# A depthwise convolution whose middle tap is added by a transfer, in an FFT mixing and gated convolution kernel

## The chip, the cores and the metric

The kernel runs on one core of a Trainium2 chip. The metric is the time of one execution on the device in microseconds, as the median of several runs. One further execution was taken with the hardware profiler; its trace is what the profile views below show.

## The reference

For each of 8 batches, the input of 3136 positions by 256 features is transformed by a two-dimensional Fourier transform, of which the real part is kept. A feed-forward block with a gate follows, all in float32:

```python
X = np.fft.fft(np.fft.fft(x, axis=1), axis=2).real      # (8, 3136, 256)
h = np.maximum(X @ w_in, 0.0)                            # (8, 3136, 1024)
conv = sum(conv_w[k] * shifted(h, k) for k in range(3))  # per feature, along the positions, zeros outside
out = (h / (1.0 + np.exp(-conv))) @ w_out                # (8, 3136, 256)
```

## The kernel before, in words

The kernel folds the sequence by the symmetries of the transform (VectorE adds and subtracts halves of the input tile `xh` into `w`), multiplies the folded input with cosine and sine tables (TensorE, PSUM tile `pd`), and gets for each batch two tables `pt` and `qt` (`PQ[b]`) of 128 rows. The transform along the features and `w_in` are multiplied into one matrix `G` at the start.

The main loop has 256 steps: 8 batches, 4 chunks of positions in a batch, 8 blocks of 128 hidden features in a chunk. A step `t` works on one block of one chunk, with positions along the free axis: 770 columns of `h` to convolve, 832 in the last chunk. A chunk holds a stretch of positions and its mirror image, since the two share products.

What one step does, in the order of the data:

- `seed` (ACT, line 748) writes a rank-one term into the PSUM tile `pa`; there are two of these tiles.
- `products` (TensorE, lines 768 to 771) multiplies `G` with `qt` into `pb` (one tile) and with `pt` onto `pa`.
- `copies` (ACT, line 784) takes `pb` with both signs into `nb`.
- `row_of` (line 762) gets a tile for `h`; in chunk 0 GpSimd sets its two edge columns to zero with a memset.
- `combine` (VectorE, line 795) adds `pa` and `nb` and cuts at zero, in two halves: that is `h`.
- `first_tap` (ACT, line 801) writes `g`, the first of the three products of the convolution.
- `tap` (VectorE, line 806) adds the second and the third product, one instruction each.
- `sigmoid` (ACT, line 821) takes `g` in two pieces.
- `gate` (lines 829 and 830) multiplies `g` by `h`: GpSimd one half of the columns, VectorE the other.
- `keep` (ACT, line 837) stores the last 64 columns of a batch in `left`, so that two batches share one matmul for them.
- `mm2` (TensorE, line 849) multiplies `g` with `w_out` and sums over the 8 blocks in the PSUM tiles `po`; after the eighth, ACT copies them to `os` and SP's queue stores them.

A step `third` (lines 754 to 756), in which VectorE has side work at the start, spares VectorE one half of `combine`: TensorE adds the sum in PSUM with one more product, ACT takes the half out (line 781), and in those steps the gate is cut 3 to 1 in place of 1 to 1 two steps ahead.

The order of work on each engine is written out by hand, in the loop at the end (lines 1016 to 1047). In cycle `t` the engines get: the sigmoid of step t-2, products and copies of t+1, the products with `w_out` of t-3, combine and first tap of t, the seed of t+2, the second and third tap of t-1 and the gate of t-2. Every engine takes its instructions in this order and waits in place for what it needs.

Side work is put into the cycles by name (`side`): the folds of the next batch on VectorE, the products with the tables on TensorE (`pd`), small edge copies on GpSimd (line 178), loads of the next batch's input. Of a batch's input, SP's queue loads two halves of 784 KB and GpSimd issues eight gathers of mirrored rows (line 131). In the first cycles the weights are turned from 64-bit to 32-bit floats on VectorE and ACT.

Of the kernel before, what the change touches and what calls it, by code (L numbers as in the profile page):

```python
# [9 lines left out]
F32 = mybir.dt.float32  # L10
I32 = mybir.dt.int32
U32 = mybir.dt.uint32
AF = mybir.ActivationFunctionType
ALU = mybir.AluOpType
# [16 lines left out]
NQ = 8  # L31
CUTS = (0, 384, 768, 1152)
BIG = 3.4028234663852886e38


@with_exitstack
def kernel(
# [10 lines left out]
    nc = tc.nc  # L48
    B, S, D = x.shape
    F = moe_w_in.shape[1]  # L50
    P = 128
# [9 lines left out]
    NF = F // P  # L61
# [6 lines left out]
    const = ctx.enter_context(tc.tile_pool(name="const", bufs=1))  # L68
# [4 lines left out]
    ebp = ctx.enter_context(tc.tile_pool(name="ebp", bufs=4))  # L73
    asp = ctx.enter_context(tc.tile_pool(name="asp", bufs=4))
    pqp = ctx.enter_context(tc.tile_pool(name="pqp", bufs=2))
    hp = ctx.enter_context(tc.tile_pool(name="hp", bufs=4))
    gp = ctx.enter_context(tc.tile_pool(name="gp", bufs=5))
    nbp = ctx.enter_context(tc.tile_pool(name="nbp", bufs=2))
    osp = ctx.enter_context(tc.tile_pool(name="osp", bufs=3))
    edp = ctx.enter_context(tc.tile_pool(name="edp", bufs=1, space=DRAM))  # L80
# [5 lines left out]
    vt = nc.vector.tensor_tensor  # L86
    gt = nc.gpsimd.tensor_tensor
    stt = nc.vector.scalar_tensor_tensor
    act = nc.scalar.activation

    def mm(o, l, r, start, stop):
        nc.tensor.matmul(o, l, r, start=start, stop=stop, skip_group_check=True)  # L92

    def spare():

        return pso.tile([P, 2, D], F32, name="po", tag="po").rearrange("p a d -> p (a d)")
# [611 lines left out]
    cw = const.tile([P, 3, NF], F32, name="cw")  # L708
# [12 lines left out]
    def column(i):  # L721

        w, p = w4[i], spare()
        for m in range(NF // 4):
            for t in range(2):
                mm(p[:, m:m + 1], w[:, t, m * P:(m + 1) * P], dm[:, t, 1, P - 1:P], t == 0, t == 1)
        nc.scalar.copy(out=ge[:, i * NF // 4:(i + 1) * NF // 4], in_=p[:, 0:NF // 4])

    def taps():
        p = spare()  # L730
        mm(p[:, 0:3 * NF], cw24[:, 0], ident, True, True)
        nc.scalar.copy(out=cw.rearrange("p k m -> p (k m)"), in_=p[:, 0:3 * NF])


    rows = out.rearrange("b s d -> (b s) d")
    hs, gs, pa, pb, po, nb = {}, {}, {}, {}, {}, {}
# [6 lines left out]
    def seed(s):  # L743

        b, c, f = s
        ch, n, fs = cut(s)
        pa[s] = psa.tile([P, 512], F32, name="pa", tag="pa")
        act(pa[s][:, 0:n], eb[b, c], AF.Copy, scale=ge[:, f:f + 1])  # L748

    def triple(s):  # L750

        return third(steps.index(s))

    def third(i):

        return 3 <= i < 12 and (i, "dve") in side

    def row_of(s):
        hs[s] = hp.tile([P, HW], F32, name="h", tag="h")
# [4 lines left out]
    def products(s):  # L764
        b, c, f = s
        ch, n, fs = cut(s)
        pb[s] = psb.tile([P, 512], F32, name="pb", tag="pb")
        mm(pb[s][:, 0:n], G[0:P - 1, 1, fs], PQ[b][1][0:P - 1, ch.k0:ch.k1], True, True)
        mm(pa[s][:, 0:n], G[:, 0, fs], PQ[b][0][:, ch.k0:ch.k1], False, not triple(s))
        if triple(s):  # L770
            mm(pa[s][:, 0:n], G[0:P - 1, 1, fs], PQ[b][1][0:P - 1, ch.k0:ch.k1], False, True)

    def copies(s):

        ch, n, fs = cut(s)
        p = pb.pop(s)
        nb[s] = nbp.tile([P, 2, HN], F32, name="nb", tag="nb")
        if triple(s):
            act(nb[s][:, 1, ch.cols], p[:, ch.cols], AF.Copy, scale=-2.0)
            row_of(s)  # L780
            act(hs[s][:, ch.front], pa[s][:, ch.fcols], AF.Relu)
        else:
            for i, cols in enumerate((ch.fcols, ch.cols)):
                act(nb[s][:, i, cols], p[:, cols], AF.Copy, scale=-1.0 if i else 1.0)  # L784

    def combine(s):

        ch, n, fs = cut(s)
        a, c = pa.pop(s), nb.pop(s)
        if not triple(s):  # L790
            row_of(s)
        h = hs[s]
        for i, (to, cols) in enumerate(((h[:, ch.front], ch.fcols), (h[:, ch.back][:, ::-1], ch.cols))):
            if i or not triple(s):
                nc.vector._custom_dve(TENSOR_ADD_SAT, out=to, in0=a[:, cols], in1=c[:, i, cols],  # L795
                                      s0=BIG, s1=0.0)

    def first_tap(s):
        n = chunks[s[1]].w - 2
        gs[s] = gp.tile([P, HW - 2], F32, name="g", tag="g")[:, 0:n]  # L800
        act(gs[s], hs[s][:, 0:n], AF.Copy, scale=cw[:, 0, s[2]:s[2] + 1])  # L801

    def tap(s, k):
        g, h, f = gs[s], hs[s], s[2]
        n = g.shape[1]
        stt(out=g, in0=h[:, k:k + n], scalar=cw[:, k, f:f + 1], in1=g, op0=ALU.mult, op1=ALU.add)  # L806

    def shares(s):


        ch = chunks[s[1]]
        w = ch.w - 2
        n = ch.rest[0] if ch.last else w
        m = n - n // (4 if third(steps.index(s) + 2) else 2)
        return slice(0, m), slice(m, n), slice(n, w)

    def sigmoid(s):

        v, p, r = shares(s)
        for c in (slice(p.start, r.stop), v):  # L820
            act(gs[s][:, c], gs[s][:, c], AF.Sigmoid)  # L821

    def gate(s):

        b, c, f = s
        g, h = gs[s], hs.pop(s)[:, 1:]
        v, p, r = shares(s)
        p = slice(p.start, r.stop)
        gt(g[:, p], g[:, p], h[:, p], op=ALU.mult)  # L829
        vt(g[:, v], g[:, v], h[:, v], op=ALU.mult)  # L830

    def keep(s):

        b, c, f = s
        r = shares(s)[2]
        if r.start < r.stop:
            nc.scalar.copy(out=left[:, f, b % 2 * LEFT:(b % 2 + 1) * LEFT], in_=gs[s][:, r])

    def mm2(s):
        b, c, f = s  # L840
        ch = chunks[c]
        tiles = [(gs[s][:, o:o + m], [(0, b, r, m)]) for o, r, m in ch.tiles]
        if ch.last and b % 2:
            tiles.append((left[:, f], [(i * LEFT, b - 1 + i, ch.rest[1], LEFT) for i in range(2)]))
        for i, (w, to) in enumerate(tiles):
            if f == 0 and i % 2 == 0:
                po[b, c, i // 2] = pso.tile([P, 2, D], F32, name="po", tag="po")
            pt = po[b, c, i // 2]
            mm(pt[:, i % 2, :], w, wout[:, f, :], f == 0 and i % 2 == 0, f == NF - 1)
            if f == NF - 1 and (i % 2 or i == len(tiles) - 1):  # L850
                del po[b, c, i // 2]
                osb = osp.tile([P, 2, D], F32, name="os", tag="os")
                for j in range(i - i % 2, i + 1):
                    nc.scalar.copy(out=osb[:, j % 2], in_=pt[:, j % 2])  # L854
                    for p0, b_, r, m in tiles[j][1]:
                        nc.sync.dma_start(out=rows[b_ * S + r:b_ * S + r + m, :], in_=osb[p0:p0 + m, j % 2])
        gs.pop(s)


    w_cv.narrow(0, 1)  # L860
    taps()
    idle = psb.tile([P, 512], F32, name="pb", tag="pb")

# [48 lines left out]
    n = chunks[0].k1  # L912
# [9 lines left out]
    steps = [(b, c, f) for b in range(B) for c in range(len(chunks)) for f in range(NF)]  # L922
    per = len(chunks) * NF
    side = {}
# [43 lines left out]
    for b in range(1, B):  # L968
# [4 lines left out]
        n = per * b - 3 - c0  # L973
        at(max(c0, per * (b - 1) + 1), "pe", begin)
        cs = [c0 + i * n // len(us) for i in range(len(us) + 1)]
        for i, u in enumerate(us):
            k = cs[i + 1] - cs[i]
# [8 lines left out]
    for b in range(1, B):  # L986
        ops, singles, pres = fold_ops(b)
        c0, n = ends[b - 1], ends[b] - ends[b - 1]
# [17 lines left out]

    LAG = 3
    n = len(steps)  # L1010
    seed(steps[0])
    seed(steps[1])
# [2 lines left out]
    column(1)  # L1015
    for t in range(n + LAG):
        def run(where):
            for fn in side.get((t, where), []):
                fn()
        if 0 <= t - 2 < n:  # L1020
            sigmoid(steps[t - 2])
        run("first")
        if t + 1 < n:
            products(steps[t + 1])
            copies(steps[t + 1])
        run("act")
        if t >= LAG:
            keep(steps[t - LAG])
        if t < n:
            combine(steps[t])  # L1030
        if t + 2 < n:
            seed(steps[t + 2])
        if t < n:
            first_tap(steps[t])

        if 0 <= t - 1 < n:
            tap(steps[t - 1], 1)
        run("dve")
        if 0 <= t - 1 < n:
            tap(steps[t - 1], 2)  # L1040
        if 0 <= t - 2 < n:
            gate(steps[t - 2])
        run("pool")
        run("load")
        if t >= LAG:
            mm2(steps[t - LAG])
        run("pe")
# [66 lines left out]
```

## Time and profile before

| | |
|---|---|
| median of 3 runs | 1200.08 us (1199.71 to 1200.8) |
| profiled execution | 1194.98 us |
| its span in the trace | 1193.2 us |
| granted clock of TensorE | 0.995 |
| busy TensorE, VectorE, ACT, GpSimd | 1152.5, 1134.9, 899.6, 405.5 us |

The span runs from the first instruction of the program to the end of the last one. Matmuls are pipelined and their ends are modelled, so that a busy TensorE is not one at its peak; the distance from one matmul's start to the next is the better measure of its pace. In the views, PE is TensorE's matmul, PEld its weight load, DVE is VectorE, ACT is ScalarE, POOL is GpSimd and SP is SyncE. An arrow behind a group of instructions names what the engine waited for before it. Line numbers are those of the kernel before.

### The profile page before, as it was taken

Reading aid. Unit: us, or ns where it says so; the run is one execution under the profiler, and the core shown is the slowest. Engines: PE = TensorE matmul, PEld = TensorE weight load, DVE = VectorE, ACT = ScalarE, POOL = GpSimd, SP = SyncE. Lnnn points to the kernel's source line nnn. Section 1 sums busy time; section 2 is a strip of 40 time slices with the busy share of each in tenths; the row PEclk is TensorE's granted clock in tenths of the full one; section 3 lists DMA queues with packets and bytes.
Section 4 is the critical chain, followed back from the end, with each engine's and each line's share of the span. In section 5 each row is a group of like instructions: output and inputs, shape, how many; then the busy total and the mean of one; then the engine's idle time right before and its main releaser. Section 6 shows DMA issues by size and latency. Waiting matters only on the chain.

```text
span 1193.2 us, 15532 instructions
## 1 busy us (share of the span) xinstructions
PE 1152.5 (97%) x4836; PEld 890.9 (75%) x4836; DVE 1134.9 (95%) x1693; ACT 899.6 (75%) x1937; POOL 405.5 (34%) x476
## 2 busy tenths in 40 slices
PE   3899999999999999999999999999999999999998
PEld 1766777678876787777778777777778777777776
DVE  6799999999999999999999999999999998999996
ACT  2377767787777777778786877888787777888885
POOL 5235524524253423344423242242312233222222
PEclk9899999999999999999999999999999999999999
DMA  7622232311032120211121020310001100110001
GB/s 179 200 17 75 77 41 74 89 40 57 13 108 59 55 61 30 73 54 61 47 75 51 15 81 27 89 47 27 27 16 39 32 27 28 47 34 27 27 27 31
DMA packets 70723, 65.16 MB, mean 55 GB/s; under 512 B 28563, under 2 KB 58535, under 8 KB 70641
## 3 DMA queue, kind: packets, MB, share of 16 engines
q1 hardware_dynamic: 64583, 51.05, 15.4%
q0 software_dynamic: 5120, 12.85, 3.7%
q8 instruction: 38, 0.62, 0.2%
q10 hardware_dynamic: 938, 0.28, 0.1%
q14 instruction: 44, 0.36, 0.1%
HBM read 38.40 MB, written 25.74 MB: 54 GB/s over the span
## 4 chain that ended last, share of the span: by engine, by line
PE 72%; DVE 16%; issue 4%; ACT 4%; DMA 2%; POOL 1%; SPq 0%; DVEq 0%; ACTq 0%; POOLq 0%
PE po L92 46%; PE pb L92 11%; PE pa L92 10%; DVE g L806 7%; PE pd L92 5%; DVE h L795 3%; DVE g L830 2%; POOL xh L131 1%; DMA tab<-dft_seq_dram 1%; ACT nb L784 1%; ACT g L821 1%; DMA out_dram<-os 1%; ACT os L854 1%; DVE w L194 1%; DMA xh<-in_x_dram 0%
## 5 line engine op out<-in xcount | busy, mean ns | idle before, releaser
L92 PE MATMUL po<-wout,g 128*128 128x256 f32 x3072 | 709.8, 381 | 10.8 <-DVE g L830 10.2
L92 PEld LDWEIGHTS po<-wout,g 128*128 128x128 f32 x3072 | 577.6, 190 | 166.3 <-DVE g L830 48.4
L806 DVE SCALAR_TENSOR_TENSOR g<-h,cw,g 128x770 f32<-128x770 f32 (+1 forms) x512 | 564.8, 1103 | 4.1 <-ACT g L801 0.9
L829 POOL TENSOR_TENSOR g<-g,h 128x385 f32<-128x385 f32 (+2 forms) x256 | 265.1, 1036 | 727.5 <-ACT g L821 550.2
L821 ACT ACTIVATE g<-g 128x385 f32<-128x385 f32 (+4 forms) x512 | 245.2, 531 | 167.9 <-DVE g L806 167.2
L784 ACT ACTIVATE nb<-pb 128x386 f32<-128x386 f32 (+2 forms) x494 | 218.6, 497 | 68.3 <-PE pb L92 66.8
L795 DVE CUSTOM_DVE_ANT_0 h<-pa,nb 128x386 f32<-128x386 f32 (+2 forms) x503 | 260.0, 556 | 1.7 <-POOL h L762 1.7
L801 ACT ACTIVATE g<-h,cw 128x770 f32<-128x770 f32 (+1 forms) x256 | 244.2, 954 | 0.0
L92 PE MATMUL pb<-qt,G 127*128 127x387 f32 (+2 forms) x512 | 214.6, 500 | 1.8 <-ACT nb L784 0.8
L92 PE MATMUL pa<-pt,G 128*128 128x387 f32 (+2 forms) x512 | 212.2, 495 | 0.3 <-ACT pa L748 0.3
L748 ACT ACTIVATE pa<-eb,ge 128x387 f32<-128x387 f32 (+2 forms) x256 | 155.3, 607 | 1.6 <-DVE h L795 1.0
L92 PEld LDWEIGHTS pa<-pt,G 128*128 128x128 f32 x512 | 97.2, 190 | 74.4 <-issue 18.1
L830 DVE TENSOR_TENSOR g<-g,h 128x385 f32<-128x385 f32 (+2 forms) x256 | 148.2, 579 | 3.4 <-ACT g L821 3.4
L131 POOL DMA_INDIRECT xh<-in_x_dram,idx x64 | 101.9, 1592 | 13.0 <-issue 9.7
L92 PE MATMUL pd<-tab,w 98*128 98x197 f32 (+2 forms) x448 | 98.5, 318 | 1.0 <-DVE w L194 1.0
L92 PEld LDWEIGHTS pb<-qt,G 127*128 127x128 f32 x512 | 91.1, 190 | 8.1 <-ACT G L717 2.0
L92 PEld LDWEIGHTS pd<-tab,w 98*128 98x128 f32 (+1 forms) x448 | 81.9, 191 | 10.8 <-issue 1.6
L854 ACT COPY os<-po 128x256 f32<-128x256 f32 x196 | 57.5, 398 | 8.7 <-DMA out_dram<-os 5.3
L156 DVE TENSOR_TENSOR xh<-xh 98x1020 f32<-98x1020 f32 (+1 forms) x32 | 39.4, 1234 | 4.0 <-DMA xh<-in_x_dram,idx 4.0
L167 DVE TENSOR_TENSOR xh<-xh 98x1024 f32<-98x1024 f32 (+1 forms) x32 | 39.9, 1246 | 0.1
L178 POOL COPY w<-xh 98x4 f32<-98x4 f32 (+1 forms) x32 | 26.9, 842 | 7.3 <-DVE xh L172 3.7
L193 DVE TENSOR_TENSOR w<-xh 98x508 f32<-98x508 f32 (+1 forms) x32 | 22.3, 698 | 0.1
(136 smaller groups left out, 376.9 us busy)
## 6 DMA issues: line engine op xcount, KB each, us to landing
out_dram<-os SPq DMA_DIRECT2D x192, 128.0 KB
xh<-in_x_dram SPq DMA_DIRECT2D x16, 784.0 KB
eb<-ed SPq DMA_DIRECT2D x16, 193.5 KB
raw<-in_moe_w_in_dram SPq DMA_DIRECT2D x4, 512.0 KB
raw<-in_moe_w_out_dram SPq DMA_DIRECT2D x1, 2048.0 KB
eb<-ed SPq DMA_DIRECT2D x8, 209.0 KB
eb<-ed SPq DMA_DIRECT2D x7, 193.0 KB
tab<-dft_seq_dram SPq DMA_DIRECT2D x2, 589.5 KB
```

Source lines behind the costliest of these rows:

```text
L92: nc.tensor.matmul(o, l, r, start=start, stop=stop, skip_group_check=True)
L131: nc.gpsimd.indirect_dma_start(out=xh[b, h][0:NP, 7 - m].rearrange("p q d -> p (q d)"), out_offset=None, in_=bass.AP(tensor=x.tensor, offs ...
L167: vt(flat(to, to + 2), flat(0, 2), flat(2, 4), op=op)
L748: act(pa[s][:, 0:n], eb[b, c], AF.Copy, scale=ge[:, f:f + 1])
L784: act(nb[s][:, i, cols], p[:, cols], AF.Copy, scale=-1.0 if i else 1.0)
L795: nc.vector._custom_dve(TENSOR_ADD_SAT, out=to, in0=a[:, cols], in1=c[:, i, cols], s0=BIG, s1=0.0)
L801: act(gs[s], hs[s][:, 0:n], AF.Copy, scale=cw[:, 0, s[2]:s[2] + 1])
L806: stt(out=g, in0=h[:, k:k + n], scalar=cw[:, k, f:f + 1], in1=g, op0=ALU.mult, op1=ALU.add)
L821: act(gs[s][:, c], gs[s][:, c], AF.Sigmoid)
L829: gt(g[:, p], g[:, p], h[:, p], op=ALU.mult)
L830: vt(g[:, v], g[:, v], h[:, v], op=ALU.mult)
L854: nc.scalar.copy(out=osb[:, j % 2], in_=pt[:, j % 2])
```

## The change

The three taps of a feature are w0, w1 and w2. At the start, w0 and w2 are divided by w1 (a w1 whose square is below 1e-36 first gets 2e-18 added). The convolution is then w1 times (w0/w1 h[-1] + h[0] + w2/w1 h[+1]). The first tap and the last tap stay where they were, on ACT and VectorE. The middle term needs no product any more: GpSimd's queue issues a transfer from SBUF to SBUF that adds `h` onto `g`, 128 rows of 770 or 832 columns. The sigmoid multiplies by w1 as it reads.

In cycle `t`, the transfer of step t is issued behind the gate on GpSimd's queue; the last tap is that of step t-2, sigmoid and gate are those of t-3, and the products with `w_out` are those of t-4. The pools of `h` and `g` get one tile more. `third` is false for every step, so no step has the extra product, and the gate is always cut 1 to 1.

```diff
-    hp = ctx.enter_context(tc.tile_pool(name="hp", bufs=4))
-    gp = ctx.enter_context(tc.tile_pool(name="gp", bufs=5))
+    hp = ctx.enter_context(tc.tile_pool(name="hp", bufs=5))
+    gp = ctx.enter_context(tc.tile_pool(name="gp", bufs=6))
...
         nc.scalar.copy(out=cw.rearrange("p k m -> p (k m)"), in_=p[:, 0:3 * NF])
+        small = const.tile([P, NF], F32, name="small")
+        vt(small, cw[:, 1], cw[:, 1], op=ALU.mult)
+        nc.vector.tensor_scalar(out=small, in0=small, scalar1=TINY * TINY, scalar2=2.0 * TINY, op0=ALU.is_lt,
+                                op1=ALU.mult)
+        vt(cw[:, 1], cw[:, 1], small, op=ALU.add)
+        nc.vector.reciprocal(out=small, in_=cw[:, 1])
+        for k in (0, 2):
+            vt(cw[:, k], cw[:, k], small, op=ALU.mult)
...
     def third(i):
 
-        return 3 <= i < 12 and (i, "dve") in side
+        return False
...
-    def tap(s, k):
-        g, h, f = gs[s], hs[s], s[2]
+    def middle(s):
+        n = gs[s].shape[1]
+        nc.gpsimd.dma_start(out=gs[s], in_=hs[s][:, 1:1 + n], accum_op=ALU.add)
+
+    def last_tap(s):
+        g, h, f, k = gs[s], hs[s], s[2], 2
         n = g.shape[1]
         stt(out=g, in0=h[:, k:k + n], scalar=cw[:, k, f:f + 1], in1=g, op0=ALU.mult, op1=ALU.add)
...
-            act(gs[s][:, c], gs[s][:, c], AF.Sigmoid)
+            act(gs[s][:, c], gs[s][:, c], AF.Sigmoid, scale=cw[:, 1, s[2]:s[2] + 1])
...
-    LAG = 3
+    LAG = 4
...
-        if 0 <= t - 2 < n:
-            sigmoid(steps[t - 2])
+        if 0 <= t - 3 < n:
+            sigmoid(steps[t - 3])
...
-        if 0 <= t - 1 < n:
-            tap(steps[t - 1], 1)
         run("dve")
-        if 0 <= t - 1 < n:
-            tap(steps[t - 1], 2)
         if 0 <= t - 2 < n:
-            gate(steps[t - 2])
+            last_tap(steps[t - 2])
+        if 0 <= t - 3 < n:
+            gate(steps[t - 3])
+        if t < n:
+            middle(steps[t])
         run("pool")
         run("load")
```

1 line of the change is left out of this document (added).

## The prediction

> **What bounds the kernel now.** I read the profile page first, then busy time by batch, then the chain of waits in one stretch, then the timeline of two steps. On the page (engine totals, the chain, the costliest groups: count, busy us, mean ns, idle before):
>
> ```profile
> PE 1152.5 (97%) x4836; PEld 890.9 (75%) x4836; DVE 1134.9 (95%) x1693; ACT 899.6 (75%) x1937; POOL 405.5 (34%) x476
> PE 72%; DVE 16%; issue 4%; ACT 4%; DMA 2%; POOL 1%; SPq 0%; DVEq 0%; ACTq 0%; POOLq 0%
> L92 PE MATMUL po<-wout,g 128*128 128x256 f32 x3072 | 709.8, 381 | 10.8 <-DVE g L830 10.2
> L806 DVE SCALAR_TENSOR_TENSOR g<-h,cw,g 128x770 f32<-128x770 f32 (+1 forms) x512 | 564.8, 1103 | 4.1 <-ACT g L801 0.9
> L829 POOL TENSOR_TENSOR g<-g,h 128x385 f32<-128x385 f32 (+2 forms) x256 | 265.1, 1036 | 727.5 <-ACT g L821 550.2
> L131 POOL DMA_INDIRECT xh<-in_x_dram,idx x64 | 101.9, 1592 | 13.0 <-issue 9.7
> ```
>
> TensorE and VectorE are both nearly full. VectorE holds the two tap products (512, 2.2 us a step); TensorE holds 72% of the chain, and its listed waits on VectorE's gate are only 10.2 us. So the question is how much of TensorE's time is VectorE's fault. The stretches below are batches 1 to 6, each from its first pb matmul to the next batch's (length; busy PE, PEld, DVE, ACT, POOL; clock; DMA share):
>
> ```profile
> 206.90:352.00 145.10, 142.74 (x602) 109.13 (x601) 142.47 (x216) 110.04 (x236) 57.54 (x62) 1.00 0.21 62
> 352.00:493.90 141.90, 140.19 (x586) 107.61 (x585) 139.22 (x216) 111.12 (x237) 49.18 (x60) 1.00 0.17 52
> 493.90:634.50 140.60, 139.59 (x590) 108.80 (x589) 138.76 (x212) 110.73 (x237) 52.25 (x58) 1.00 0.20 61
> 634.50:773.60 139.10, 138.25 (x586) 108.28 (x585) 135.37 (x205) 109.26 (x234) 45.38 (x56) 1.00 0.17 52
> 773.60:912.20 138.60, 138.32 (x585) 108.11 (x584) 137.51 (x210) 110.96 (x236) 40.71 (x52) 1.00 0.11 35
> 912.20:1048.90 136.70, 136.70 (x583) 108.13 (x582) 124.77 (x179) 108.14 (x231) 35.91 (x41) 1.00 0.10 31
> ```
>
> Batch 6 has no folds left for VectorE (124.8 of 136.7 us busy), and TensorE is never idle: that is what a batch costs when TensorE alone sets the pace. The others differ by VectorE's load. The chain of waits in batch 6 gives one step of TensorE:
>
> ```profile
> 953.20 2.59 PE po L92 x12
> 959.91 0.35 PE pd L92 x2
> 960.26 0.65 PE pb L92 x2
> 960.92 0.66 PE pa L92 x2
> ```
>
> A step is 3.90 us, or 4.25 with two pd matmuls. That is a floor no relief of VectorE goes under; the change can win only the distance to it.
>
> **The change part by part.** Times are those of the profiled execution (1194.98 us, span 1193.2); the median of the runs, 1200.08, is 5.1 above it, which I add at the end.
>
> *One tap leaves VectorE.* 256 products of 1.103 us are 282 us off VectorE, which leaves it near 72%. What is on the path is the excess of batches 1 to 5 over batch 6. An odd batch also multiplies left-over rows: 16 matmul records at 2.59/12 = 0.216 us, 3.5 us. Against 136.7 (even) and 140.2 (odd) the excesses are 4.9, 5.2, 0.4, 2.4 and 0 us: **-12.9**. Next to be late is TensorE itself.
>
> *The third product of early steps goes* (nine steps took an extra pa matmul pair to spare VectorE):
>
> ```profile
> L92 PE MATMUL pa<-qt,G 127*128 127x386 f32 x10 | 4.1, 486 | 0.0
> L92 PE MATMUL pa<-qt,G 127*128 127x387 f32 x8 | 3.3, 487 | 0.0
> ```
>
> 18 records at 0.33 us of issue (half of the 0.65 pair above): **-5.9**. VectorE takes nine combines of 0.55 us back, covered by the 34 us of taps that it loses in that batch. Of batch 0's other waits I take half of the page's 10.2 us on the gate: **-4.5** (0 to -10).
>
> *One step more of lag.* One more step at the start has no po matmuls: about 3.9 us long (ACT and VectorE set it), 1.3 us of TensorE work: **+2.5**. At the end nothing: po matmuls follow the last pa back to back for five steps,
>
> ```profile
> 1172.35 0.87 PE L92 MATMUL pa<-pt,G 128*128 128x418 f32 x2
> 1187.73 0.59 PE L92 MATMUL po<-wout,left 128*128 128x256 f32 x2
> ```
>
> 15 us, against 0.88+1.01+0.93+5.7+1.01+0.94+1.04 = 11.5 us from the last pa to its gate (copies, combine, first tap, transfer, last tap, sigmoid and gate, by the rows here and below). Six tiny VectorE instructions in the set-up: 0 to +1, I take **+0.3**; the buffers cost no time. The sigmoid's scale per partition: the first tap, which has one, runs 0.93 us for 770 columns, the sigmoid 0.94 for its two halves (below); nothing.
>
> *The transfer.* No accumulating transfer is in this trace. Two steps of the timeline show where it must fit (start, us):
>
> ```profile
> 700.59 0.94 ACT L821 ACTIVATE g<-g 128x385 f32<-128x385 f32 x2 [0.99 <-DVE g L806]
> 700.77 0.82 PE L92 MATMUL pb<-qt,G 127*128 127x387 f32 x2
> 700.95 1.01 DVE L795 CUSTOM_DVE_ANT_0 h<-pa,nb 128x386 f32<-128x386 f32 x2
> 701.63 0.88 ACT L784 ACTIVATE nb<-pb 128x386 f32<-128x386 f32 x2
> 702.39 0.59 ACT L748 ACTIVATE pa<-eb,ge 128x387 f32<-128x387 f32 x1
> 702.90 0.93 ACT L801 ACTIVATE g<-h,cw 128x770 f32<-128x770 f32 x1
> 703.94 1.01 DVE L806 SCALAR_TENSOR_TENSOR g<-h,cw,g 128x770 f32<-128x770 f32 x1
> ```
>
> The new order is first tap (step t), transfer, last tap two steps on, sigmoid three steps on, and behind it on ACT the copies, the seed and the first tap of t+3. From first tap to first tap is three steps, of which 0.93+1.01+0.94+0.88+0.59 = 4.4 us are work. At 4.25 us a step, 8.4 us remain for issue and landing. VectorE waits at the last tap with the gate and the next combine queued behind it, and TensorE's PSUM behind those. GpSimd waits at the transfer for the first tap, with its memset, gathers, edge copies and the next gate's half queued behind it. The nearest transfers are the gathers that GpSimd issues (min/median/max), and the DMA queues' totals (packets, MB, share of 16 engines):
>
> ```profile
> L131 POOL DMA_INDIRECT xh<-in_x_dram,idx x64: 964/1522/4370, 2.1 to 784.6; - x64
> DMA to landing us min/median/max: 3.1/3.7/9.1
> q1 hardware_dynamic: 64583, 51.05, 15.4%
> q0 software_dynamic: 5120, 12.85, 3.7%
> ```
>
> A gather (12.85 MB/64 = 201 KB) lands 3.7 us after its issue begins. q0 held the engines 0.037x16x1193 = 706 us for 12.85 MB: 55 ns a KB. The transfer is 394 KB, 24.6 KB an engine: 1.35 us if it costs as a copy; 4.05 if two reads and a write go one after another. I take two passes, 2.7: landing is then 3.7 + 2.0 = 5.7 us of 8.4, hidden, and with the other traffic (0.21x145/32 = 0.95 us a step, 0.4 late) the engines hold 3.1 to 3.65 of 4.25 us. Collisions with 784 KB loads: 0 to +10, I take **+2**. [...]
>
> *GpSimd's queue.* Each step now has the gate's half (1.04), the issue, and in 52 of the 256 steps a gather (1.59; the first 12 lie before them): at an issue of 1.5 about 2.9 us of 4.25. I price the issue at 1.0 to 1.6 us by the gather, unknown beyond. But chunk 0 (64 steps) has a tight ring: the memset of h's edges of t+1 stands behind the issue of t, and the combine of t+1 waits for it. Combine 1.01, seed 0.59, first tap 0.93, memset 0.1 and some 0.25 of hand-over are 2.9 us plus the issue: 4.4 at 1.5, just over a step. This row is what such waits cost before:
>
> ```profile
> DVE h L795 <- POOL h L762: 1.7, 3, 1.0
> ```
>
> 13 gathers fall between those memsets and add 1.5 us each; about 2.5 us a batch are absorbed by the double PSUM. Issue 0.7: +2; 1.0: +9; 1.5: +16. I take **+8**.
>
> Sum: -12.9 -5.9 -4.5 +2.5 +0.3 +2 +8 = -10.5: 1184.5 for the profiled execution, 1189.5 for the median. Its own range is 1165 (batch 0 fully cured, no collision, batches to the floor of 135.5) to 1197.
>
> **The rivals.**
>
> *The transfer holds the DMA engines.* At 4.05 us plus 0.8 (batches 0 to 4) or 0.45 (5 to 7), steps last 4.85 and 4.5 us: 160 and 96 steps are 1208, plus 53.5 before the first pb and 22 after the last, 1284, as median about 1290. It decides from 3.3 us on. For it: nothing here bounds the price. Against: one pass costs 1.35.
>
> ```profile
> 53.54 1.66 PE L92 MATMUL pb<-qt,G 127*128 127x386 f32 x2 [0.46 <-DVE win L622]
> 101.48 4.37 POOL L131 DMA_INDIRECT xh<-in_x_dram,idx  x1 [0.18 <-issue]
> ```
>
> *The issue is dear.* From about 1.8 us the ring of chunk 0 eats the gain. At 2.5: 8 steps of 1.15 too long less 2.5 absorbed are 6.7 a batch, 54 in all, and 20 for gathers: about 1252. For it: one gather held GpSimd 4.37 us. Against: the mean is 1.59. [...]
>
> *The landing is late.* At the longest, 9.1 us, in place of 5.7 with the issue in it, a step is (4.4+9.1)/3 = 4.5 us: 53.5+1152+22, about 1233. It decides from 8.4.
>
> *Nothing moves.* TensorE is 97% busy, and the ring at an issue of 1.6 us with the fill takes back the 23 us that taps, third product and batch 0 give: 1198 to 1202.
>
> **How the numbers follow.** Forecast 0.42; engines 0.20; issue 0.20; landing 0.10; nothing 0.08. A measurement tells 0.2% (2.4 us) from no change. The likeliest gives 1189. Leaving out the far end of engines and issue (0.15) and the gain beyond the floor (0.05), the range is 1165 to 1390, where each transfer would hold the engines 4.4 us. The likeliest case's own range, 1165 to 1197, stands beside it. Faster 0.42, same 0.08, slower 0.50.
>
> **What would show it.** Right: VectorE near 72%, batch 1 at 140 us, no third product, last tap without a wait on the transfer, chunk 0 the slowest chunk with the combine waiting on the memset. Wrong: last tap waits on the transfer in most steps (engines above 80% in DMA share: first rival; below 60%: landing), or an issue over 1.8 us on GpSimd.

## The result and the profile after

The changed kernel takes 1203.92 us (median of 13 runs, 1201.24 to 1206.74) against 1200.08 us (median of 13 runs beside them, 1192.85 to 1201.39): a ratio of 1.0040 with a 95% interval of 1.0026 to 1.0054. It is slower by 0.4%, where the forecast was 1189, faster by 0.9%. The time lies in the range given, and outside the range of the likeliest case. A ratio here compares a kernel with the runs of the kernel before that were taken beside it, and so differs a little from the quotient of two medians.

The profiled execution took 1203.03 us (span 1201.3), near the median. That of before, at 1194.98, was one of its short ones, so the difference of the two traces (8 us) is twice that of the medians; the section on the hardware returns to this. Line numbers of after are one higher up to line 700, and 9 to 13 higher in the main loop. The engine totals, the chain, the costliest groups and the transfers' queue on the page of after:

```profile
PE 1149.4 (96%) x4818; PEld 891.4 (74%) x4818; DVE 942.8 (78%) x1452; ACT 945.1 (79%) x1937; POOL 585.8 (49%) x732
q0 software_dynamic: 41984, 115.83, 50.9%
PE 73%; DVE 8%; ACT 7%; issue 5%; POOL 4%; DMA 2%; DVEq 0%; ACTq 0%; POOLq 0%; SPq 0%
L93 PE MATMUL po<-wout,g 128*128 128x256 f32 x3072 | 708.4, 380 | 14.8 <-DVE g L843 14.6
L814 POOL DMA_DIRECT2D g<-h x256 | 227.6, 889 | 510.3 <-ACT g L810 198.9
L834 ACT ACTIVATE g<-g,cw 128x385 f32<-128x385 f32 (+2 forms) x512 | 291.4, 621 | 86.5 <-DVE g L819 85.5
L819 DVE SCALAR_TENSOR_TENSOR g<-h,cw,g 128x770 f32<-128x770 f32 (+1 forms) x256 | 293.5, 1147 | 32.5 <-DMA g<-h 32.5
```

VectorE has indeed lost a tap: 95% busy before, 78% now, and its share of the chain is halved, from 16 to 8%. But TensorE's waits on the gate (the last figures of the L93 line) rose from 10.2 to 14.6 us. Batches 1 to 6 in the windows of after (length; busy PE, PEld, DVE, ACT, POOL; clock; DMA share; GB/s):

```profile
209.20:353.10 143.90, 141.21 (x599) 108.94 (x598) 118.71 (x187) 117.69 (x238) 74.55 (x93) 1.00 0.70 150
353.10:495.20 142.10, 139.60 (x587) 108.48 (x587) 117.16 (x180) 115.30 (x236) 80.85 (x92) 1.00 0.68 144
495.20:636.10 140.90, 138.36 (x587) 108.69 (x587) 110.20 (x176) 115.58 (x235) 73.25 (x91) 1.00 0.70 150
636.10:776.70 140.60, 138.99 (x588) 108.62 (x587) 113.67 (x177) 116.27 (x236) 68.93 (x89) 1.00 0.68 144
776.70:916.80 140.10, 137.83 (x585) 108.03 (x584) 112.69 (x177) 116.33 (x236) 65.96 (x86) 1.00 0.61 127
916.80:1054.40 137.60, 137.27 (x583) 108.31 (x582) 99.53 (x148) 113.45 (x231) 57.41 (x73) 1.00 0.61 124
```

VectorE has 25 to 38 us a batch to spare, and yet the six batches together are 845.2 us against 842.0 before. Something else holds the steps up. The list of waits of after (waiter, releaser: us in total, times, longest) names two candidates in the loop, and one in the set-up:

```profile
DVE h L804 <- POOL h L771: 81.2, 57, 3.2
DVE g L819 <- DMA g<-h: 32.5, 35, 3.7
DVE small L735 <- ACT cw L733: 9.7, 1, 9.7
```

The combine waits for the memset of `h`'s edges 57 times in the 64 steps of chunk 0, 81.2 us against 1.7 before. Not all of it is lost time: an engine may wait while TensorE, which holds 73% of the chain, still has work. The last tap waits for the transfer in 35 of 256 steps only. And in the set-up VectorE's first instruction for the division waits 9.7 us.

The theory after the result, A: the relief is real, but the ring of chunk 0 (transfer's issue, memset, combine, first tap, next issue) and the division at the head of VectorE's queue eat it. The rivals: B, the transfers themselves cost it, by their engines or their landing; C, VectorE never set the time, so that there was nothing to win.

### The profile page after: what moved, and what is told of

It reads as the page before. It is cut to its first block, busy times and chain, and to the rows that moved or that the text cites. A ratio compares the mean times of both kernels' runs of the same rounds, so it can differ in the third digit from the quotient of the medians.

```text
span 1201.3 us, 16042 instructions
## 1 busy us (share of the span) xinstructions
PE 1149.4 (96%) x4818; PEld 891.4 (74%) x4818; DVE 942.8 (78%) x1452; ACT 945.1 (79%) x1937; POOL 585.8 (49%) x732
## 4 chain that ended last, share of the span: by engine, by line
PE 73%; DVE 8%; ACT 7%; issue 5%; POOL 4%; DMA 2%; DVEq 0%; ACTq 0%; POOLq 0%; SPq 0%
PE po L93 47%; PE pb L93 11%; PE pa L93 10%; PE pd L93 5%; DVE g L819 3%; ACT g L834 2%; DMA g<-h 2%; POOL xh L132 2%; ACT nb L793 2%; POOL g L814 1%; DVE h L804 1%; ACT os L867 1%; ACT g L810 1%; DVE xh L168 1%; DVE g L843 1%
## 5 line engine op out<-in xcount | busy, mean ns | idle before, releaser
L93 PE MATMUL po<-wout,g 128*128 128x256 f32 x3072 | 708.4, 380 | 14.8 <-DVE g L843 14.6
L93 PEld LDWEIGHTS po<-wout,g 128*128 128x128 f32 x3072 | 579.2, 190 | 165.6 <-DVE g L843 39.8
L814 POOL DMA_DIRECT2D g<-h x256 | 227.6, 889 | 510.3 <-ACT g L810 198.9
L834 ACT ACTIVATE g<-g,cw 128x385 f32<-128x385 f32 (+2 forms) x512 | 291.4, 621 | 86.5 <-DVE g L819 85.5
L804 DVE CUSTOM_DVE_ANT_0 h<-pa,nb 128x386 f32<-128x386 f32 (+3 forms) x512 | 264.8, 557 | 87.6 <-POOL h L771 81.2
L819 DVE SCALAR_TENSOR_TENSOR g<-h,cw,g 128x770 f32<-128x770 f32 (+1 forms) x256 | 293.5, 1147 | 32.5 <-DMA g<-h 32.5
L842 POOL TENSOR_TENSOR g<-g,h 128x385 f32<-128x385 f32 (+1 forms) x256 | 283.5, 1108 | 48.0 <-ACT g L834 46.4
L793 ACT ACTIVATE nb<-pb 128x386 f32<-128x386 f32 (+3 forms) x512 | 225.7, 494 | 84.5 <-PE pb L93 84.1
L93 PE MATMUL pb<-qt,G 127*128 127x387 f32 (+2 forms) x512 | 214.2, 499 | 3.7 <-ACT nb L793 2.8
L93 PE MATMUL pa<-pt,G 128*128 128x387 f32 (+2 forms) x512 | 212.2, 495 | 1.4 <-ACT pa L757 1.4
L843 DVE TENSOR_TENSOR g<-g,h 128x385 f32<-128x385 f32 (+1 forms) x256 | 166.4, 650 | 12.2 <-ACT g L834 12.1
L93 PEld LDWEIGHTS pa<-pt,G 128*128 128x128 f32 x512 | 96.4, 189 | 76.3 <-issue 16.7
L93 PE MATMUL pd<-tab,w 98*128 98x197 f32 (+2 forms) x448 | 98.7, 318 | 3.0 <-POOL w L181 1.5
L93 PEld LDWEIGHTS pb<-qt,G 127*128 127x128 f32 x512 | 91.0, 191 | 10.5 <-ACT nb L793 4.0
L132 POOL DMA_INDIRECT xh<-in_x_dram,idx x64 | 84.3, 1317 | 18.8 <-issue 16.1
L93 PEld LDWEIGHTS pd<-tab,w 98*128 98x128 f32 (+1 forms) x448 | 81.7, 191 | 13.8 <-ACT pa L757 2.9
L157 DVE TENSOR_TENSOR xh<-xh 98x1020 f32<-98x1020 f32 (+1 forms) x32 | 44.3, 1391 | 0.0
L227 DVE SCALAR_TENSOR_TENSOR w<-w,turn,rt 98x256 f32<-98x256 f32 x28 | 12.3, 481 | 23.1 <-ACT rt L221 23.1
```

The costliest lines, as they stand in the source:

```text
L132: nc.gpsimd.indirect_dma_start(out=xh[b, h][0:NP, 7 - m].rearrange("p q d -> p (q d)"), out_offset=None, in_=bass.AP(tensor=x.tensor, offs ...
L814: nc.gpsimd.dma_start(out=gs[s], in_=hs[s][:, 1:1 + n], accum_op=ALU.add)
L834: act(gs[s][:, c], gs[s][:, c], AF.Sigmoid, scale=cw[:, 1, s[2]:s[2] + 1])
```

## The experiments

The ratio to the kernel before, with its 95% interval, stands first in each result; 0.1% is 1.2 us.

**The division behind batch 0's folds.** The edit puts the lines of the division into a function that is called after the loop of folds:

```diff
         nc.scalar.copy(out=cw.rearrange("p k m -> p (k m)"), in_=p[:, 0:3 * NF])
+
+    def divide():
         small = const.tile([P, NF], F32, name="small")
...
+    divide()
     odds = [us[j] for j in (0, 1, 5, 6)]
```

> The changed kernel with the division of the taps moved on VectorE's queue from ahead of batch 0's folds to behind them; nothing else. Theory (a wait at the head of VectorE's queue: in the changed kernel the folds start 8.3 us later, because the first division waits 9.7 us for ACT's copy of the taps, and TensorE's granted clock then lies at 0.5 from 43.7 to 60.8 us): folds start near 8.3 us as before, the first pb matmul comes near 53.5 us in place of 60.3, and the time is 5 to 8 us below the changed kernel's 1203.9, that is 1196 to 1199. Rival (the set-up's difference is chance of loads and clock, from run to run): the first pb stays anywhere between 53 and 60 us and the time stays within 2 us of 1203.9.

Measured: 1.0002 [0.9981, 1.0023], 1197.04 us: by the ratios 4.6 us faster than the change, uncertain by 3. The time agrees with A; the expected start of the first pb at 53.5 us does not, it was 58.5 in the profiled execution (one of the longer, 1199.77 us). The granted clocks of its runs, 0.990 to 0.994, are about those of the change, 0.988 to 0.994, so that the mean clock doesn't explain the gain.

**The memset ahead of the transfer.** `row_of` of the next step, with its memset, goes to GpSimd before the transfer of this one:

```diff
-        if not triple(s):
-            row_of(s)
...
+    row_of(steps[0])
     for t in range(n + LAG):
...
+        if t + 1 < n:
+            row_of(steps[t + 1])
         if t < n:
             middle(steps[t])
```

> The changed kernel with the memset of h's edges of step t+1 issued ahead of the transfer of step t on GpSimd's queue (its tile is taken one cycle earlier); nothing else. Theory (ring of chunk 0): the 81 us in which VectorE's combine waits for the memset fall under 10 us, chunk 0 of batches 1 to 6 loses the 14.8 us by which it stands above TensorE's own pace, of which 10 to 13 come off the time: 1191 to 1194. Rival (TensorE's pace hides it, the waits of the combine are slack): the waits vanish, the time stays within 2 us of 1203.9.

Measured: 0.9936 [0.9912, 0.9960], 1189.29 us: by the ratios 12.5 us off the change. From its waits:

```profile
DVE h L802 <- POOL h L771: 15.2, 11, 2.0
```

The wait fell from 81.2 to 15.2 us, not quite to the 10 expected; the median lies a little below the 1191 to 1194 expected. In the two traces chunk 0 of batches 1 to 6, from its first pb matmul to that of chunk 1, takes 222.4 us in the change and 208.8 here, so the gain comes from where the ring was.

**Both**, the two edits above together.

> Both moves together. If both theories hold and add up: 1203.9 - 6.5 - 12 = 1185, between 1182 and 1189, which is faster than the kernel before by 1.0 to 1.5%. If only one holds: 1191 to 1199. If neither: 1202 to 1206.

Measured: 0.9895 [0.9868, 0.9921], 1184.82 us. The two repairs add up (1.04% and 0.38% alone, 1.45% together), and the idea is then worth 1%.

**The kernel before without the second product.**

```diff
-        if 0 <= t - 1 < n:
-            tap(steps[t - 1], 1)
         run("dve")
```

> The kernel before without its second tap on VectorE; it leaves out the middle term of the convolution. Nothing of the transfer, of the division or of the longer lag. Theory (VectorE's two taps cost the prediction's 12.9 us in batches 1 to 5 and some 4.5 in batch 0, the rest is TensorE's own): 15 to 20 us below the kernel before, 1180 to 1185. Rival (TensorE paces the kernel and hides VectorE): within 4 us of the kernel before.

Measured: 0.9828 [0.9797, 0.9860]. C falls: VectorE's tap was worth 1.7%, 20.6 us, and TensorE's waits on the gate go from 10.2 to 1.2 us (groups by line):

```profile
L92 PE MATMUL po<-wout,g 128*128 128x256 f32 x3072 | 705.0, 379 | 1.3 <-DVE g L830 1.2
```

**The repaired kernel without the transfer.** From the version with both repairs:

```diff
-        if t < n:
-            middle(steps[t])
         run("pool")
```

> The version with both moves (1184.8 us), without the transfer; it leaves out the middle term of the convolution. It stands 7.6 us above the kernel before without its second tap (1177.2). Theory (the transfer itself costs the rest: last taps that wait for it in 45 steps for 39 us, gathers held up on GpSimd's queue, steps of batches 1 and 2 with excess): 4 to 6 us less, 1179 to 1181. Rival (the longer lag, the set-up and its clock cost the rest, and the transfer is hidden): 1183 to 1186.

Measured: 0.9842 [0.9809, 0.9875]. The transfers cost the difference to 0.9895, 0.53%, 6 us by the ratios and 3.3 by the medians of the two (1184.82 and 1181.54). The intervals just touch, so this is a size with a large error; B holds for a few us and not for the loss.

**The kernel before without the third product.**

```diff
-        return 3 <= i < 12 and (i, "dve") in side
+        return False
```

> The kernel before with the third product taken out of the nine early steps (third returns False); nothing else. Theory (the prediction's price of 5.9 us of TensorE time holds only where VectorE has room, and in the kernel before it has none): VectorE takes 9 combines of 0.55 us more and the gate's cut falls back to halves, so the time is within 3 us of the kernel before, 1197 to 1202. Rival (5.9 us of TensorE are on the path in any case): 1192 to 1195.

Measured: 1.0003 [0.9983, 1.0022]: nothing. The same stretch, batch 0, in the windows of the kernel before:

```profile
53.20:208.00 154.80, 147.27 (x612) 109.52 (x612) 150.04 (x231) 114.88 (x257) 63.28 (x62) 0.99 0.31 64
```

and of this kernel:

```profile
53.20:208.00 154.80, 140.96 (x590) 105.00 (x591) 149.99 (x239) 113.89 (x256) 52.24 (x63) 1.00 0.32 63
```

TensorE has 6.3 us less to do and the batch is no shorter (153.4 before, 154.8 here). In the chain of before from 66 to 110 us, a part of that batch, TensorE isn't what sets the pace:

```profile
by line: DVE g L806 23.8%; PE po L92 12.4%; DVE g L830 8.7%; issue 6.8%; DVE wout L625 5.8%; DVE h L795 5.3%; DVE raw L632 5.2%; PE pa L92 5.0%; ACT os L854 3.7%; DVE wout L635 3.4%; ACT g L821 3.3%; PE pb L92 3.0%; ACT L821 2.9%; DVE xh L1
```

**The wait alone, in the kernel before.** One product of 8 columns after ACT's copy of the taps, at the place of the division:

```diff
         nc.scalar.copy(out=cw.rearrange("p k m -> p (k m)"), in_=p[:, 0:3 * NF])
+        small = const.tile([P, 3, NF], F32, name="small")
+        vt(small[:, 0], cw[:, 1], cw[:, 1], op=ALU.mult)
```

> The kernel before with one added instruction of 0.17 us on VectorE, at the place of the division: a product of 8 columns of the taps, which waits for ACT's copy of them and whose result nothing uses. Theory (a wait at the head of VectorE's queue ahead of batch 0's folds): the folds start at 16 to 18 us in place of 8.3, and the time is 4 to 8 us above the kernel before. Rival (the tables' loads cover the folds' delay, and chance of the clock made the difference): within 2 us of the kernel before.

Measured: 1.0017 [1.0003, 1.0032], 1201.11 us. The median moved by about the rival's amount and missed the theory's. The timeline of its set-up (start, duration, in brackets the idle time before) shows the wait all the same:

```profile
15.89 0.17 DVE L734 TENSOR_TENSOR small<-cw 128x8 f32<-128x8 f32 x1 [9.80 <-ACT cw L732]
16.00 2.35 DVE L156 TENSOR_TENSOR xh<-xh 98x1020 f32<-98x1020 f32 x2
```

The first fold starts at 16.0 us, not at 8.3. All 12 of its runs were granted a clock of 0.991 to 0.993, while most of those of the kernel before beside them had 0.988 to 0.990. Taken by clock, seven runs of before at 0.991 to 0.993 have a median of 1197.55, so that the wait costs 3.6 us at an equal clock. That selection was made after the result; it is a reading and not a test. So the wait alone is shown to delay the folds, and not to cost what moving the division gained.

**The gate before the last tap on VectorE**, in the repaired kernel: does the last tap, which waits for the transfer, hold the gate up behind it?

```diff
-        if 0 <= t - 2 < n:
-            last_tap(steps[t - 2])
         if 0 <= t - 3 < n:
             gate(steps[t - 3])
+        if 0 <= t - 2 < n:
+            last_tap(steps[t - 2])
```

> The version with both moves, with VectorE's half of the gate of step t-3 put ahead of the last tap of step t-2. Theory (TensorE's 7.2 us of waits on VectorE's gate come from gates queued behind a last tap that waits for its transfer): those waits fall to under 2 us and the time by 2 to 4 us, 1181 to 1183. Rival (the gate then waits for the sigmoid at the head of the queue and holds the last tap back, which holds the next sigmoid): the same or up to 5 us above 1184.8.

Measured: 0.9951 [0.9929, 0.9973], slower than with both repairs by 6.7 us by the ratios and 10 by the medians. TensorE's waits on the gate did fall, from 7.2 to 0.9 us, as the theory had it, but the time rose. From the waits of the repaired kernel:

```profile
ACT g L834 <- DVE g L819: 82.4, 101, 3.7
DVE g L819 <- DMA g<-h: 39.1, 45, 4.2
DVE g L843 <- ACT g L834: 16.7, 17, 3.5
```

and of this one:

```profile
ACT g L834 <- DVE g L819: 144.2, 149, 4.2
DVE g L843 <- ACT g L834: 65.9, 93, 4.4
DVE g L819 <- DMA g<-h: 8.5, 8, 3.0
```

The wait on the transfer falls from 39.1 to 8.5 us, and the gate and the sigmoid wait longer by 49 and 62. The order of the change was the better one.

**One step more of lag alone**, in the kernel before without the second product (pools of 5 and 6 as in the change):

```diff
-    LAG = 3
+    LAG = 4
...
-            sigmoid(steps[t - 2])
+            sigmoid(steps[t - 3])
...
-            tap(steps[t - 1], 2)
+            tap(steps[t - 2], 2)
...
-            gate(steps[t - 2])
+            gate(steps[t - 3])
```

> The kernel before without its second tap (1177.2 us; it leaves out the middle term), with the changed kernel's order: last tap two steps back, sigmoid and gate three, the products with w_out four, one tile of h and g more. Theory (the longer lag costs its prologue, a step without those products, and no more): 2 to 4 us more, 1179 to 1181, with 3 us of it after the last pb matmul and as much lost at the start. Rival (work put off to the end is not lost): within 1 us of 1177.

Measured: 0.9857 [0.9823, 0.9891], 0.29% or 3.5 us more than without the lag (0.9828); the intervals overlap, so that this doesn't decide. The stretch from the last pb to the end grew from 21.6 to 24.6 us, as it did in the change. But from the first pb to the last the trace with the lag is 2.4 us shorter, so that from the first pb to the end the two differ by 0.6 us (1118.6 and 1119.2). That speaks for the rival: the work that moved to the end is missing before it.

**The third product back in the repaired kernel**, where VectorE has time; the gate is still cut in halves, and `row_of` of the next step stands ahead of its `products`:

```diff
-        return False
+        return 3 <= i < 12 and (i, "dve") in side
...
         if t + 1 < n:
+            row_of(steps[t + 1])
             products(steps[t + 1])
```

> The version with both moves (1184.8 us), with the third product back in the nine early steps (the gate cut in halves throughout, and the tile of h of t+1 taken ahead of its products). Theory (with VectorE relieved, the third product is only work for TensorE, as the prediction had it): 4 to 6 us more, 1189 to 1191. Rival (as in the kernel before, where taking it out changed nothing: early steps wait for something else): within 2 us of 1184.8.

Measured: 0.9902 [0.9864, 0.9939] beside 0.9895 without it. The interval is wide, but the traces say the same: from the first pb to the end 1125.5 us with the third product and 1125.9 without. Again nothing.

**Half as much transfer again**, in the repaired kernel: a second accumulating transfer of half the columns, into a spare tile that nobody reads.

```diff
             middle(steps[t])
+            again(steps[t])
```

> The version with both moves, with a second accumulating transfer in each step, of half the columns, into a spare tile that nothing reads. The trace of the changed kernel gives 2.2 us of the DMA engines a step; now 3.3, beside 0.95 (early) to 0.4 us (late) of other traffic, of a step of 4.25. Theory (the engines decide from about 3.3 us on, and GpSimd has room for one issue more): 1190 to 1215, with early batches above 145 us and late ones near 138. Rival (landing decides sooner, since both transfers share the engines): steps of all batches above 4.4 us, 1215 to 1260.

Measured: 1.0109 [1.0075, 1.0144], 2.1% more. From the page, and the landing of the first transfer:

```profile
q0 software_dynamic: 78848, 167.32, 76.5%
DMA to landing us min/median/max: 3.7/4.6/9.1
```

The landing hardly moved at the median (4.1 in the change, 4.6 here), but the transfers now hold the engines for 3.4 us of a step of 4.4 (0.765x1201.8 less 44 us, by 256), with the loads on top. So half as much again was dear where the first 2.2 us were cheap. The time and the late batches are as expected; the early ones, 143.0 and 144.2 us in batches 1 and 2, stay under the 145 expected. That the engines did it isn't shown. The edit also adds an issue of 1.17 us to GpSimd's queue in each step; the last tap's waits on the transfer fell from 39.1 to 32.2 us, while those of the combine on the memset rose from 14.3 to 27.4, and the last tap itself takes 1341 ns in the mean, against 1161 in the repaired kernel.

**Idle matmuls before the set-up's last part**, to keep TensorE's clock up, in the repaired kernel, in the change, and in the kernel before:

```diff
                     w_out.load(nc.sync)
+    keep_on([idle] * 3)
     mend_row(0, half)
```

> The version with both moves, with three pairs of idle matmuls (12 records of 512 columns, 2.6 us at full clock) where TensorE waits 2.3 us in the set-up near 41 us, ahead of the stretch of half clock (42.0 to 59.1 us in that version's trace). Theory (the granted clock falls because TensorE stood idle there): the stretch of half clock after 40 us goes or is under 7 us long, the first pb matmul comes near 53 to 55 us, the time is 4 to 7 us less, 1178 to 1181. Rival (the clock falls for another reason): half clock stays, the time stays at 1183 to 1187.

> The changed kernel as it is, division ahead of the folds and memset behind the transfer, with the three pairs of idle matmuls where TensorE stood idle near 41 us. Theory (the division costs through the half clock of 17 us that follows that idle time): the half clock after 40 us shrinks to under 7 us, and the time falls by 4 to 7 us, to about the kernel before (1196 to 1200), as much as moving the division behind the folds gave. Rival (the folds' delay costs by itself): the half clock shrinks, the time stays within 2 us of 1203.9.

> The kernel before with the same three pairs of idle matmuls. Theory (the kernel before, too, has a set-up at half clock in most of its executions, which is why its times spread from 1192 to 1202 us and its profiled execution, with 3.4 us of half clock there, is a fast one): 1190 to 1194, spread under 4 us. Rival (the spread has another cause): median and spread as before, 1197 to 1201, 1192 to 1202.

Measured: the repaired kernel 0.9869 [0.9842, 0.9895] (1180.67 us, the fastest of the kernels that leave nothing out, though its interval overlaps that without them); the change 1.0004 [0.9981, 1.0027] (1197.59); the kernel before 0.9943 [0.9929, 0.9956] (1192.99, and all five runs within 0.6 us). The idle matmuls take 2.73 us in each of the three traces. The granted clocks of the runs are 0.994 to 0.998, 0.995 to 0.999 and 0.996 to 0.997, against 0.990 to 0.993, 0.988 to 0.994 and 0.988 to 0.997 without them. All three medians fall, that of the repaired kernel within the error. With the idle matmuls the change is slower than before by 4.6 us by the medians (1197.59 and 1192.99) and by 7.3 by the ratios, without by 3.8 and 4.8: the half clock (0.50 from 45 to 57 us in the trace of the change) is a cost of its own, which both pay, and not why the change lost.

## Why the prediction was wrong

The runs in a chain, each against the one before it, give the terms beside those forecast (us). The column of ratios is uncertain by 3 to 6 us in each row, and its sum comes out by construction. The column of traces takes the time from the first pb matmul to the end of the span, one execution each, and so leaves out the set-up; there the kernel before takes 1139.7 us, the links of the chain 1118.6, 1119.2, 1122.2, 1125.9 and 1139.5, and the change 1141.0. Three of these loops were profiled again with idle matmuls in the set-up, and differ by 1.0 to 1.6. By the two sums, some 3.6 of the 4.9 us lie in the set-up.

| step of the prediction | forecast | by ratios | by traces | from |
|---|---|---|---|---|
| a tap off VectorE, with batch 0's gate waits | -17.4 | -20.6 | -21.1 | before without the second product |
| one step more of lag | +2.5 | +3.5 | +0.6 | lag alone |
| left over (lag alone to repaired without transfer; the sigmoid's scale and the third product are in it) | | -1.8 | +3.0 | |
| the transfer: engines, landing, collisions | +2 | +6.4 | +3.7 | repaired kernel with and without it |
| ring of chunk 0 | +8 | +12.8 | +13.6 | both repairs against the division alone |
| division in the set-up | +0.3 | +4.6 | +1.5 | change against the division moved |
| third product gone, measured apart | -5.9 | 0 | 0 to +1 | before without it; repaired kernel with it |
| sum | -10.5 | +4.9 | +1.3 | |

The mechanisms were foreseen, and three of the signs that were to show it right came: no third product, few waits for the transfer, chunk 0 held by the memset. Two did not: VectorE is 78% busy and not 72, batch 1 takes 143.9 us and not 140. The direction was wrong because terms of the sum were: by the ratios the third product (-5.9 forecast, 0 measured) and the ring (+8, +12.8) make some 11 us of the 15 between forecast and result. That the time lies in the wide range is luck: its upper part was there for dear transfers and issues, and neither came.

- **The relief** was right, and a little small: in the traces 14.6 us in batches 1 to 5 (forecast 12.9) and 6.6 in batch 0 (4.5). C is out.
- **The third product** failed as a step: I counted TensorE's work (18 records) as time. The nine steps lie where VectorE, ACT and the weights' conversion set the pace, which the chain of that stretch would have shown before. Taken out of that stretch, 6.3 us of TensorE's work gave nothing (1.0003).
- **The lag** has three microseconds in the tail (21.6 to 24.6), which I had put at nothing, and gains most of them back before it. Its +2.5 isn't borne out by the traces (0.6), and the ratios are too coarse to tell.
- **The transfer** was sized well by itself. It lands 4.1 us after its issue begins (forecast 5.7), the issue takes 0.89 us (1.0 to 1.6), and it holds each engine 2.2 us: 0.509x1201.3 less 0.037x1193 us of q0, by 256 (forecast 2.7, two passes at the gathers' 55 ns a KB; no run shows that it is two). The rivals of engines (from 3.3 us on), issue (1.8) and landing (8.4) were therefore out. The measured 2.2 is 1.64 times the 1.35 of a copy by the gathers' price. The +2 for collisions was nearer to +3 to +6.
- **The ring** is the largest loss. Its length was right; what failed is how much of it TensorE would not feel. Two turns in chunk 0 of batch 5 of the change, in the timeline (other rows left out):

```profile
788.18 1.02 DVE L804 CUSTOM_DVE_ANT_0 h<-pa,nb 128x385 f32<-128x385 f32 x2 [2.77 <-POOL h L771]
789.24 0.59 ACT L757 ACTIVATE pa<-eb,ge 128x386 f32<-128x386 f32 x1 [1.64 <-DVE h L804]
789.76 0.93 ACT L810 ACTIVATE g<-h,cw 128x770 f32<-128x770 f32 x1
789.89 0.59 PE L93 MATMUL pd<-tab,w 98*128 98x197 f32 x2 [0.65 <-ACT pa L757]
790.99 0.92 POOL L814 DMA_DIRECT2D g<-h  x1 [1.90 <-DVE g L819]
792.21 1.06 POOL L132 DMA_INDIRECT xh<-in_x_dram,idx  x1 [0.30 <-issue]
793.26 0.12 POOL L771 MEMSET h<- 128x2 f32 x1
793.42 1.02 DVE L804 CUSTOM_DVE_ANT_0 h<-pa,nb 128x385 f32<-128x385 f32 x2 [2.21 <-POOL h L771]
795.00 0.92 ACT L810 ACTIVATE g<-h,cw 128x770 f32<-128x770 f32 x1
796.22 0.92 POOL L814 DMA_DIRECT2D g<-h  x1 [1.90 <-PE pa L93]
796.83 0.43 POOL L771 MEMSET h<- 128x2 f32 x1
797.03 2.86 PE L93 MATMUL po<-wout,g 128*128 128x256 f32 x12 [1.00 <-DVE g L843]
797.30 1.02 DVE L804 CUSTOM_DVE_ANT_0 h<-pa,nb 128x385 f32<-128x385 f32 x2 [0.32 <-POOL h L771]
```

  The first turn, combine to combine, takes 5.24 us and has a gather of the next batch's input (1.06 us, and 0.30 ahead of it) between issue and memset. The second has none and takes 3.88. In both the issue starts 0.30 us behind the end of the first tap, whatever the brackets name. Where nothing else comes between, the turns of chunk 0 take 3.83 us, which is the prediction's 2.9 and the measured issue, and less than TensorE's step of 4.2 there. With a gather they take 5.24 to 5.58, and there are 13 such turns, as the prediction had counted: 4, 1, 4, 2 and 2 in batches 1 to 5. Together they exceed 13 of TensorE's steps by 14 us.

  From this the prediction took off some 2.5 us a batch, to be absorbed by the double PSUM (there are two tiles `pa`). Against the version with the memset ahead, batches 1 to 5 of the change take 2.7, 0.6, 3.4, 2.2 and 3.1 us more. In batches 1 and 3, where the gathers' turns exceed TensorE's steps by 4.3 us each, 1.6 and 0.9 were absorbed; in batches 4 and 5 (2.0 each) nothing was, and turns that wait for ACT's other work add to the loss. Batches 6 and 7 have no gathers in chunk 0; the combine waits for the memset there too (11.7 us in batch 7), and they lose 0.3 and nothing. Batch 0 loses 2.6, with side work and no gather in its turns. That the gathers make most of the loss is read from the traces: no run moved them alone.
- **The division** was priced by the durations of "six tiny VectorE instructions", and what moving it gained is more. The set-up of before, in its timeline:

```profile
8.31 1.22 DVE L156 TENSOR_TENSOR xh<-xh 98x1020 f32<-98x1020 f32 x1 [2.23 <-DMA xh<-in_x_dram,idx]
```

  and of after:

```profile
15.58 0.17 DVE L735 TENSOR_TENSOR small<-cw 128x8 f32<-128x8 f32 x1 [9.71 <-ACT cw L733]
16.59 2.34 DVE L157 TENSOR_TENSOR xh<-xh 98x1020 f32<-98x1020 f32 x2
```

  VectorE stands still for 9.7 us with the folds of batch 0 queued behind. How this becomes 4.6 us stays open. The same wait alone in the kernel before cost 1 to 2 us. In the two traces TensorE reaches the last pause of the set-up at 40.5 us before and 40.7 in the change, since in the kernel before a load of the tables holds it up as well (to 29.8 us, by the chain of waits); the rest of the 6.7 us by which the first pb is later (60.28 against 53.54) comes with the half clock behind that pause (0.50 from 45 to 57 us; the same 32 matmuls take 9.02 us there and 4.85 before). With idle matmuls, at a mean clock of 0.88 between 39 and 57 us in place of 0.63, the timeline of the change has its first pb at

```profile
58.98 0.92 PE L93 MATMUL pb<-qt,G 127*128 127x386 f32 x2 [0.46 <-ACT G L718]
```

  and that of the repaired kernel at

```profile
49.92 1.50 PE L93 MATMUL pb<-qt,G 127*128 127x386 f32 x2 [0.46 <-ACT G L718]
```

  and the kernel before at 52.53: there the wait shows. Over all 16 traces, in the nine with a mean clock of 0.52 to 0.69 between 39 and 57 us the first pb comes at 60.0 to 60.3 us with a wait at the head of VectorE's queue and at 55.8 to 60.1 without; in the seven with 0.88 to 1.00 at 59.0 with it (one trace) and at 49.9 to 53.5 without. These are single executions, and no test of their own.

The rival "nothing moves" (1198 to 1202) was nearest in mechanism, a ring that takes back the gain, but it needed an issue of 1.6 us; the real ring took back most of it at 0.89.

## What to carry to other kernels

The work moved off the busiest engine was paid for here in the queue where its replacement is issued (12.8 us by the ratios). So list, in order, what stands behind the new instruction on that queue and who waits for that, and close the loop through every engine, with what stands between its links only now and then, such as a gather. Before part of such a loop is written off as absorbed, look for a trace that shows it. Count a removed instruction only in stretches that its engine sets. An instruction in the set-up can cost more than its duration: here its place was worth some 4.6 us, in a way that stays open. Here two moved lines, the memset ahead of the transfer and the division behind the folds, turned 0.4% slower into 1% faster.

## What the hardware showed unexpectedly

**The clock in the set-up.** The same 32 matmuls stand in the set-up of each kernel. In the timeline of before, and the window of 45 to 51 us (the granted clock is the third figure from the end):

```profile
43.60 4.85 PE L92 MATMUL po<-tab,w 99*128 99x99 f32 x32
45.00:51.00 6.00, 5.75 (x35) 4.79 (x34) 4.51 (x11) 2.32 (x6) 5.21 (x7) 1.00 1.01 373
```

The same two of the change:

```profile
43.80 9.02 PE L93 MATMUL po<-tab,w 99*128 99x99 f32 x32
45.00:51.00 6.00, 6.00 (x24) 6.00 (x24) 4.50 (x11) 1.86 (x4) 5.18 (x7) 0.50 0.98 354
```

And of the kernel before with idle matmuls:

```profile
43.04 4.85 PE L92 MATMUL po<-tab,w 99*128 99x99 f32 x32
45.00:51.00 6.00, 5.77 (x34) 4.75 (x33) 4.93 (x11) 1.77 (x5) 4.90 (x7) 1.00 0.90 329
```

Ahead of this work TensorE pauses for 2.29 us in the change and before alike. In the change a clock of 0.50 follows (45 to 57 us), and so it does with the division moved, behind the same pause; before, the clock stays at 1.00 up to 51 us, and 0.72 is the mean of the next 6. So the pause alone doesn't decide it, and what does is not shown. Over 73 runs of the kernel before, the time falls with the mean granted clock (correlation -0.95): about 1200.3 us in the 40 runs at 0.990 or less, 1192.8 in the 13 at 0.997 or more. That is where the 5.1 us come from by which its profiled execution, at 0.995, was below the median, and which the prediction added without a reason.

**The sigmoid with a scale per partition** takes 621 ns for a half (531 before), 46 us in all on ACT (page of after, L834, against L821 of before). It is the scale and not the transfer: over all its sizes it takes 623 ns in the repaired kernel with the transfer and without it, and 530 in the kernel before without the third product, which has the same three sizes and no scale. I had forecast nothing; what it costs in time was not tried (ACT's share of the chain rose from 4 to 7%).

**VectorE beside the transfers** is slower in its last tap: over both sizes it takes 1043 ns in the repaired kernel without the transfer, 1161 with it, 1341 with half as much transfer again. Its gate is slower as well, 646 ns at 385 columns in the change against 574 before, but that isn't the transfer: over both sizes the gate takes 671 without it and 682 with it in the repaired kernel, 650 in the change. So VectorE is busy 77% of the repaired kernel without the transfer and 81% with it, against the 72% of the forecast. Whether the transfers' issue or their traffic slows the last tap was not tried.
